# A fused attention and long-convolution kernel: sixteen transfers change from GpSimd's DMA queue to SyncE's

## The chip, the cores and the metric

The kernel runs on one core of a Trainium2 chip. The metric is the device time of one execution in microseconds. The engines are TensorE (PE; its weight loads are PEld), VectorE (DVE), ScalarE (ACT), GpSimd (POOL) and SyncE (SP). SP computes nothing here: it only waits and issues DMA transfers.

## The reference

Two independent blocks work on sequences of 2048 rows and 512 columns, and their results stand side by side in the output of 2048 x 1024.

```
A: qkv = x @ wqkv, 32 heads of 16
   a   = concat_heads(softmax(q k^T / 4) v) @ wo
B: k_shift = causal 4-tap filter of k, channel by channel
   kv  = k_shift * v
   y   = causal convolution of kv with ssm_k over all 2048 lags (by FFT in the reference) + kv * ssm_D
   b   = q * y
out = concat([a, b], axis=-1)
```

## The kernel before

The attention runs as a stream of chunks of two or three score blocks (128 keys by 512 queries). PE writes the scores (line 791), ACT takes the exponential of two or three blocks at once (line 798), and PE multiplies the result with v (line 866). Every second chunk or so one block's exponential is computed on DVE and POOL instead: DVE makes the integer part (line 817), POOL a linear term from it (line 290, into `EM` or `WKV`), and DVE three more passes (lines 826 and 827). Line 826 waits for POOL's result.

Between the chunks PE computes the long convolution as matmuls with Toeplitz tiles (line 998). Each of 512 channels has one tile `WR` of 128 x 2048, read from the scratch tensor `kz_scratch` (512 KB each). Fourteen tiles are held at a time. Four channels make one group ("quad"), 128 quads in all. When PE has finished quad n, SP may issue the four loads that overwrite its tiles, those of the channels 14 to 17 beyond the quad's first. So SP waits for PE once in four loads, and issues in the order of the program.

Each time 32 channels are done, PE turns the result and DVE multiplies it with q into `QN` (line 1038). `QN` holds one half of the channels: after eight turns it is stored (the first half of output B), and after that store has landed the second half of q is fetched into the same tile. The second half is stored near the end.

The attention's output projection (line 940) runs for each block of 512 queries once its heads are done. DVE copies each of its four 128 x 512 results to `OUTA` (line 952), a ring of three, and a DMA stores it (`op_out`). So a copy waits until the store three before it has landed. The last four results are stored otherwise (`op_out_end`), by SP and ACT, from `QT`. The weights of the projection are fetched into half of `WKV` at about 155 us (`load_wop`), once PE has done the last use of the weights that lay there.

All DMA transfers go through the helper `dma(eng, dsem, outp, inp, deps)`, whose first argument is the engine that waits for `deps` and issues; the profile gives each of them line 367. The order on every engine is fixed when the program is built. A planner with costs chooses the order of DVE's jobs; a store is appended to its issuing engine's list when the DVE job that makes its data is placed.

Of the kernel before, what the change touches and what calls it, by code (L numbers as in the profile page):

```python
# [13 lines left out]
D = 512  # L14
# [17 lines left out]
R_A = 3  # L32
# [139 lines left out]
def bass_concat_heads__mha_block__ssm_conv_h3__prompt_kernel(  # L172
# [12 lines left out]
    x2, q2, k2, v2, out2 = A_x[0], B_q[0], B_k[0], B_v[0], out[0]  # L185
# [8 lines left out]
    def sem(name):  # L194
        return enter(nc.semaphore(name))

    def sb(name, shape, dt=BF16):
        return enter(nc.sbuf_tensor(name, shape, dt))
# [10 lines left out]
    QN = sb("QN", [128, NB, 256])  # L209
# [7 lines left out]
    OUTA = sb("OUTA", [128, R_A, D])  # L217
# [10 lines left out]
    def xn(t):  # L228
# [5 lines left out]
    WOP = WKV[:, 0, :, :]  # L234
# [14 lines left out]
    pe, act, dve, pool, sp = [Eng(sem(n), *k) for n, k in (("s_pe", (170.0,)), ("s_act", (100.0,)), ("s_dve", (-10.0, -85.0)),  # L249
                                                           ("s_pool", ()), ("s_sp", ()))]  # L250
# [89 lines left out]
    def pe_op(fn, deps, mms):  # L340
        advance(pe.t)
        return pe.op(fn, [force(d) for d in deps], cost=Mm(*mms))

    def dve_op(fn, deps=(), cost=692.0):
        return dve.op(fn, [force(d) for d in deps], cost=cost)
# [3 lines left out]
    def dve_job(fn, deps, cost=692.0, slack=900.0, then=None, two=False):  # L349
        if dyn[0]:  # L350
            j = job(fn, deps, cost, pe.t + slack + cost, then)
            j.two = two
            return j
        h = dve_op(fn, deps, cost)
        if then:
            then(h)
        return h

    def full(n, k):
        return [("full", 0, n)] * k  # L360

    def dma(eng, dsem, outp, inp, deps=(), transpose=False):
        h = dsem.add()

        def fn(e):
            f = e.dma_start_transpose if transpose else e.dma_start
            f(outp, inp).then_inc(dsem.sem, 16)  # L367
        eng.op(fn, deps, inc=False)
        return h
# [5 lines left out]
    d_tap, d_kz, d_kzw, d_wo = [DmaSem(sem(n)) for n in ("d_tap", "d_kz", "d_kzw", "d_wo")]  # L375
    d_q = [DmaSem(sem(f"d_q{i}")) for i in range(2)]
    d_outB = [DmaSem(sem(f"d_outB{i}")) for i in range(2)]
    d_outE = DmaSem(sem("d_outE"))
    d_outA = [DmaSem(sem(f"d_outA{i}")) for i in range(R_A)]
# [212 lines left out]
    def kv_chunk(j):  # L592
        b = kvbuf[kv_buf[j]]
        st = {}

        def tap(m):
            in1 = TB[:, m:m + 1, :].broadcast_to([128, 2, D])
            st[m] = dve_job(lambda e: e.tensor_tensor(b[m], b[m], in1, ALU.mult),
                            [h_kv[(j, 0)], h_kv[(j, 1)], h_tb[m]], 750.0, 3000.0)

        def add(m):
            st["a"] = dve_job(lambda e: e.tensor_tensor(b[3], b[3], b[m], ALU.add), [st[m], st[3], st.get("a")], 750.0, 3500.0)

        def last():
            def then(h):
                h_kvfree[j] = h
                nxt = {4: 1, 3: None, 2: 0}.get(j, j - 3)
                if nxt is not None and nxt >= 0:
                    load_kv(nxt)
                for d in {6: (0, 1), 5: (2, 3), 4: (4, 11), 3: (8, 9, 12, 13), 1: (5, 6, 7)}.get(j, ()):  # L610
                    load_wr(d, [h])
                if j == 5:
                    load_qn(0, [h_kzt[0]], 4, NB)
                    line[0] += 5000.0
                elif j == 0:
                    start_conv(h)
            for i in range(2):
                dve_job(lambda e, i=i: e.tensor_tensor(KV[:, :, NB - 1 - 2 * j - i, :], quads(b[3][:, i, :]), quads(b[4][:, i, :]), ALU.mult),  # L618
                        [st["a"], h_xt[0]], 460.0, 4000.0 + i, then if i else None)
        return [lambda m=m: tap(m) for m in (3, 2)] + [lambda: add(2), lambda: tap(1), lambda: add(1),  # L620
                                                       lambda: tap(0), lambda: add(0), last]
# [60 lines left out]
    for c in range(4):  # L682
        h = turn_first([c], 2, h_xn[0])
        src = PS[:, first_bank[c], :].bitcast(BF16)[:, 0:512]
        if c == 1:
            hh = act.op(lambda e, c=c, src=src: e.activation(xT[:, c, 0:512], src, ACT.Copy), [h], cost=515.0)
        else:
            hh = dve_op(lambda e, c=c, src=src: e.tensor_copy(xT[:, c, 0:512], src), [h], 390.0)
# [237 lines left out]
    h_outa = {}  # L926
    op_count = [0]
    h_wop = [None]

    def load_wop(h_last):  # L930
        h_wop[0] = dma(pool, d_wo, WOP, A_wo.rearrange("(o p) f -> p o f", p=128), [h_last])

    def op_mm(qb, t, j0, j1, bank):
        dd = [bank_free[bank] if j0 == 0 else None, h_wop[0]]
# [10 lines left out]
    def op_out(qb, t, bank, h, slack):  # L945
        i = op_count[0]
        op_count[0] += 1
        r0 = qb * QB + t * 128

        def store(hh):  # L950
            h_outa[i] = dma(pool, d_outA[i % R_A], out2[r0:r0 + 128, 0:D], OUTA[:, i % R_A, :], [hh])
        bank_free[bank] = dve_job(lambda e: e.tensor_copy(OUTA[:, i % R_A, :], PS[:, bank, :]),  # L952
                                  [h, (lambda: h_outa.get(i - R_A, WAIT)) if i >= R_A else None], slack=slack, then=store)
        h_op[(qb, t)] = h
# [11 lines left out]
    h_wr, h_wrfree, h_qn = {}, {}, {}  # L966
# [11 lines left out]
        h_wr[d] = dma(sp, d_wr[r], WR[:, r, :], src, deps)  # L978

    def load_qn(i, deps, t0, t1):  # L980
        h_qn[i] = dma(pool, d_q[0], QN[:, t0:t1, :],
                      q2[128 * t0:128 * t1, 256 * i:256 * i + 256].rearrange("(t p) d -> p t d", p=128), deps)

    def conv_lags(qd, n0, n1):
# [34 lines left out]
    def conv_turn(b, bank, slack):  # L1019
        pbf = PS[:, bank, :].bitcast(BF16)  # L1020

        def fn(e):
            ins = None
            for k in range(4):
                ins = e.transpose(pbf[:, 128 * k:128 * k + 128], YB[:, b % 2, 128 * k:128 * k + 128], IDN[:, :])
            return ins
        h = pe_op(fn, [bank_free[bank], h_yb_in[b], h_idn], full(128, 4))
        h_yb[b] = h
        sl = b // 8
        yv = bass.AP(tensor=pbf.tensor, offset=pbf[:, NB - 1:NB].offset, ap=[pbf.ap[0], [-1, NB], [NB, CHB]])  # L1030
        qv = QN[:, :, CHB * (b % 8):CHB * (b % 8) + CHB]

        def store(hh):
            dst = out2[:, D + 256 * sl:D + 256 * (sl + 1)].rearrange("(t p) c -> p t c", p=128)
            ho = dma(pool, d_outB[0], dst, QN[:, :, :], [hh])
            if sl == 0:
                dve_later.append((len(chunks) + 14, lambda: load_qn(1, [ho], 0, NB)))
        bank_free[bank] = dve_job(lambda e: e.tensor_tensor(qv, yv, qv, ALU.mult), [h, lambda: h_qn.get(sl, WAIT)],
                                  slack=slack, then=store if b % 8 == 7 else None)
# [16 lines left out]
    def start_conv(h):  # L1056
        h_kvc[0] = h
        state["started"] = True
        load_wr(10, [h])
        load_qn(0, [h], 0, 4)  # L1060
        now = at_of(h)
        state["dma"] = max(line[0], now) + 5000.0
        state["wr"] += [now - 1000.0, max(line[0], now) + 2000.0, state["dma"] - 1400.0]
        state["dma"] -= 1400.0
# [16 lines left out]
    def run_unit(T, kind, u):  # L1081
        bank = 3 * (T % 2) + 2
        late = at_of(h_exp[T]) - pe.t - 800.0
        if kind == "u":
            state["u"] += 1
            evac_unit(u, bank, pe_unit(u, bank), slack=late - (Q_FIRST if u[0] == "q" else 0.0))
            if u[0] == "q":
                flow["half"] = max(flow["half"], T + Q_GAP)
            if u == ("k", 3, 3):
                load_wop(pe_last())  # L1090
        elif kind == "turn":
            state["turned"] += 1
            conv_turn(u, bank, late)
            if u == 7:
                state["dma"] += 8000.0
                state["wr"] = [t + 8000.0 if t > at_of(h_exp[T]) else t for t in state["wr"]]
        else:
            state["op"] += 1
            op_out(*u, bank, op_mm(*u, 0, 4, bank), slack=late)
# [303 lines left out]
```

## Time and profile before

| what | us |
|---|---|
| median of 3 runs | 847.1 |
| lowest and highest run | 843.85, 848.3 |
| time of the profiled execution | 848.2 |
| span of the profiled execution (first to last instruction) | 846.4 |
| ACT busy | 819.2 (97%) |
| DVE busy | 798.4 (94%) |
| PE busy | 719.9 (85%) |
| POOL busy | 290.6 (34%) |

In the profile, "idle before, releaser" names what ended an engine's idle time. A row of the waits reads: who waited, for whom, microseconds in total, times, longest. A row of the timeline reads: start, length, engine, line, operation, and in brackets the idle time ahead of it and what ended that. "SPq" is SP's list of instructions. "Landing" is the time from a DMA's issue to the last of its data.

### The profile page before, as it was taken

The page shows a single profiled execution, that of the slowest core. Times are in us where ns is not written, and L with a number is a line of the kernel's source. Part 1 is how long each engine was busy: PE and PEld are TensorE (multiplying, and loading weights), DVE is VectorE, ACT ScalarE, POOL GpSimd, SP SyncE. Part 2 cuts the span into 40 slices and gives each one's busy share as a digit, 9 for nine tenths or more (in the row PEclk, how much of TensorE's full clock was granted, in tenths as well). Part 3 has the DMA queues.
Part 4 walks back from the last instruction along what each step waited for, and adds up shares of the span by engine and source line. Part 5 has one row for each costly group of instructions (what it writes and reads, how often), then busy time and mean ns, then how long its engine had stood idle before and what let it go on. Part 6 is the DMA issues. An engine that isn't in the chain of part 4 may idle for free.

```text
span 846.4 us, 29917 instructions
## 1 busy us (share of the span) xinstructions
PE 719.9 (85%) x13144; PEld 310.1 (37%) x13144; DVE 798.4 (94%) x1346; ACT 819.2 (97%) x732; POOL 290.6 (34%) x323
## 2 busy tenths in 40 slices
PE   8999888888888888888888888888888988888897
PEld 3322333433343343333333333333333343333332
DVE  3998899999999999999999899999999999999996
ACT  6998999999999999999999899999999999999997
POOL 3232233334333333333333433333332334333431
PEclk9999999999999999999999999999999999999999
DMA  9878699999999999999998999999999999999810
GB/s 325 302 266 291 219 405 351 382 407 406 387 351 389 387 408 382 386 359 389 386 381 303 374 365 407 366 409 377 359 343 363 374 411 384 380 395 387 342 51 26
DMA packets 88867, 295.69 MB, mean 349 GB/s; under 512 B 11173, under 2 KB 19362, under 8 KB 88482
## 3 DMA queue, kind: packets, MB, share of 16 engines
q1 hardware_dynamic: 82818, 280.00, 87.5%
q0 software_dynamic: 3776, 12.58, 4.2%
q8 instruction: 105, 1.72, 0.8%
q10 hardware_dynamic: 2144, 1.18, 0.5%
q14 instruction: 24, 0.20, 0.1%
HBM read 287.31 MB, written 6.42 MB: 347 GB/s over the span
## 4 chain that ended last, share of the span: by engine, by line
ACT 71%; PE 13%; DVE 12%; issue 2%; DMA 1%; POOL 1%; ACTq 0%; DVEq 0%
ACT PT L798 71%; PE PS L791 5%; PE PS L866 2%; DVE PTD L827 2%; DVE EM L826 2%; DVE EI L817 2%; PE PS L521 2%; DVE WKV L826 2%; PE PS L998 1%; PE PS L940 1%; DMA WKV<-in_A_wqkv_dram 1%; DVE OUTA L952 1%; PE PS L507 1%; PE PS L514 1%; DMA QT<-in_B_k_dram 1%
## 5 line engine op out<-in xcount | busy, mean ns | idle before, releaser
L798 ACT ACTIVATE PT<-PS 128x1024 bf16<-128x1024 f32 (+1 forms) x726 | 815.6, 1328 | 16.4 <-PE PS L791 14.8
L791 PE MATMUL PS<-QT,KTo 32*128 32x512 bf16 x2048 | 287.4, 387 | 113.3 <-ACT PT L798 92.8
L998 PE MATMUL PS<-WR,KVP 128*30 128x128 bf16 (+15 forms) x8192 | 258.7, 222 | 4.7 <-issue 4.2
L998 PEld LDWEIGHTS PS<-WR,KVP 128*29 128x29 bf16 (+15 forms) x8192 | 178.2, 95 | 79.7 <-issue 40.4
L290 POOL TENSOR_SCALAR EM<-EI 128x512 f32<-128x512 uint16 x131 | 126.9, 969 | 224.3 <-DVE WKV L826 114.8
L290 POOL TENSOR_SCALAR WKV<-EI 128x512 f32<-128x512 uint16 x130 | 125.9, 969 | 208.8 <-DVE EM L826 100.3
L866 PE MATMUL PS<-PT,VAF 128*32 128x512 bf16 x1787 | 188.6, 394 | 1.8 <-issue 0.7
L817 DVE TENSOR_SCALAR EI<-PS 128x512 int32<-128x512 f32 x261 | 177.3, 679 | 7.0 <-PE PS L791 6.7
L826 DVE SCALAR_TENSOR_TENSOR EM<-EM 128x512 f32<-128x512 f32 x262 | 175.0, 683 | 2.3 <-POOL EM L290 2.0
L826 DVE SCALAR_TENSOR_TENSOR WKV<-WKV 128x512 f32<-128x512 f32 x260 | 173.1, 682 | 2.0 <-POOL WKV L290 1.8
L791 PEld LDWEIGHTS PS<-QT,KTo 32*128 32x128 bf16 x2048 | 71.8, 91 | 275.3 <-ACT PT L798 218.2
L827 DVE SCALAR_TENSOR_TENSOR PTD<-EI,EM 128x512 uint16<-128x512 int32 x131 | 89.1, 681 | 0.4
L827 DVE SCALAR_TENSOR_TENSOR PTD<-EI,WKV 128x512 uint16<-128x512 int32 x130 | 88.2, 679 | 0.3
L866 PEld LDWEIGHTS PS<-PT,VAF 128*32 128x32 bf16 x1787 | 47.4, 93 | 109.1 <-issue 99.0
L866 PE MATMUL PS<-PTD,VAF 128*32 128x512 bf16 x261 | 79.2, 394 | 0.3
L1120 PE MATMUL PS<-IDN,ZER 128*32 128x512 bf16 x396 | 44.1, 382 | 0.0
L892 DVE STREAM_TRANSPOSE DT<-PS 128x512 f32<-128x512 f32 x31 | 22.1, 712 | 8.4 <-PE PS L866 8.2
L866 PEld LDWEIGHTS PS<-PTD,VAF 128*32 128x32 bf16 x261 | 19.8, 95 | 19.6 <-issue 8.1
L542 DVE TENSOR_TENSOR QT<-PS,MSK 128x1024 bf16<-128x1024 f32 x15 | 18.3, 1222 | 4.0 <-PE PS L507 3.9
L521 PE MATMUL PS<-WKV,xT 128*128 128x512 bf16 x64 | 19.2, 384 | 0.1
L367 POOL DMA_DIRECT2D out_dram<-OUTA x12 | 7.1, 593 | 34.8 <-DVE OUTA L952 34.8
L367 POOL DMA_DIRECT2D WR<-in_B_k_dram x15 | 11.0, 737 | 22.8 <-DVE KVP L618 14.8
(80 smaller groups left out, 295.2 us busy)
## 6 DMA issues: line engine op xcount, KB each, us to landing
WR<-kz_scratch SPq DMA_DIRECT2D x512, 512.0 KB, 8.0
WR<-in_B_k_dram POOLq DMA_DIRECT2D x15, 256.0 KB, 7.4
kz_scratch<-WR SPq DMA_DIRECT2D x4, 544.0 KB, 6.6
out_dram<-QN POOLq DMA_DIRECT2D x2, 1024.0 KB, 7.9
QT<-in_B_k_dram POOLq DMA_DIRECT2D x7, 256.0 KB, 6.2
out_dram<-OUTA POOLq DMA_DIRECT2D x12, 128.0 KB, 5.7
WR<-in_B_v_dram SPq DMA_DIRECT2D x5, 256.0 KB, 8.5
WR<-in_B_k_dram SPq DMA_DIRECT2D x5, 256.0 KB, 10.4
```

Of the source, the lines that this page charges most:

```text
L290: q.h = pool.op(lambda e: e.tensor_scalar(UB[m % len(UB)], f, PA, PB, ALU.mult, ALU.add), [h, fx.h, free], cost=Beside((h[0], h[1] + 1)))
L521: return e.matmul(PS[:, bank, :], lhsT=xT[:, dc, kt * 128:(kt + 1) * 128], rhs=WV[:, dc, :], start=(dc == 0), stop=(dc == 3))
L542: hh = dve_job(lambda e: e.tensor_tensor(QT[:, qb % 2, 2 * o:2 * o + 2, :], src, MSK[:, :, 0:1].broadcast_to([128, 2, QB]), ALU.mult), [h, ...
L791: ins = e.matmul(PS[:, bank, :], lhsT=KTo[32 * s:32 * s + 32, g // 2, kt * 128:(kt + 1) * 128], rhs=QT[32 * s:32 * s + 32, qb % 2, g, :], ...
L798: h_exp[T] = act.op(lambda e: e.activation(PT[:, T % R_PT, 0:n * QB], PS[:, banks[0]:banks[0] + n, :].rearrange("p b f -> p (b f)"), ACT.E ...
L817: h_fix[i] = job(lambda e: e.tensor_scalar(ei, PS[:, bank, :], FIX_LO, FIX_ADD, ALU.max, ALU.add), [h, h_pair.get(i - 4)], 692.0, end)
L826: js.append(job(lambda e, c=c: e.scalar_tensor_tensor(u, u, c, u, ALU.add, ALU.mult), [js[-1]], 693.0, due + 700.0 * (len(js) - 3)))
L827: js.append(job(lambda e: e.scalar_tensor_tensor(PTD[:, i % 4, :].bitcast(UINT16), ei, 2.0 ** -9, u, ALU.mult, ALU.add), [js[2], (lambda: ...
L866: ins = e.matmul(PS[32 * s:32 * s + 32, pvb(qb * NG + g), :], lhsT=VAF[:, kt, h * VW:h * VW + 32], rhs=rhs, start=first[b], stop=last[b], ...
L892: h_t = dve_job(lambda e: e.transpose(out=dt, in_=PS[:, pvb(n), :]), [h, h_mult.get(n - 2 if n == 2 else n - 1) if n != 1 else None], 717. ...
L998: ins = e.matmul(PS[32 * c:32 * c + m * NB - n, BGB, 128 * kk:128 * kk + 128], lhsT=KVP[:, o:o + 4 * (m * NB - n) - 3:4], rhs=WR[:, d % R_ ...
L1120: ins = e.matmul(PS[32 * s:32 * s + 32, pvb(n), :], lhsT=ZER[:, 0:32], rhs=IDN[:, :].rearrange("p (a f) -> p a f", a=1).broadcast_to([128, ...
```

## The change

Fourteen stores (twelve of `OUTA`, two of `QN`), the fetch of the second half of q and the fetch of the projection's weights are issued by SP instead of POOL. The first half of q stays with POOL. The second fetch gets a semaphore of its own. Both halves of `QN` are still stored on the same semaphore.

```diff
     def load_wop(h_last):
-        h_wop[0] = dma(pool, d_wo, WOP, A_wo.rearrange("(o p) f -> p o f", p=128), [h_last])
+        h_wop[0] = dma(sp, d_wo, WOP, A_wo.rearrange("(o p) f -> p o f", p=128), [h_last])
...
         def store(hh):
-            h_outa[i] = dma(pool, d_outA[i % R_A], out2[r0:r0 + 128, 0:D], OUTA[:, i % R_A, :], [hh])
+            h_outa[i] = dma(sp, d_outA[i % R_A], out2[r0:r0 + 128, 0:D], OUTA[:, i % R_A, :], [hh])
...
     def load_qn(i, deps, t0, t1):
-        h_qn[i] = dma(pool, d_q[0], QN[:, t0:t1, :],
+        h_qn[i] = dma(sp if i else pool, d_q[i], QN[:, t0:t1, :],
                       q2[128 * t0:128 * t1, 256 * i:256 * i + 256].rearrange("(t p) d -> p t d", p=128), deps)
...
             dst = out2[:, D + 256 * sl:D + 256 * (sl + 1)].rearrange("(t p) c -> p t c", p=128)
-            ho = dma(pool, d_outB[0], dst, QN[:, :, :], [hh])
+            ho = dma(sp, d_outB[0], dst, QN[:, :, :], [hh])
```

The instructions of PE, ACT and DVE keep their order; POOL's and SP's change. On POOL, at about 250 us, where the first four results of the projection are stored (`out_dram<-OUTA`), among the linear terms (`EM<-EI`, `WKV<-EI`):

```order
-L290 TENSOR_SCALAR WKV<-EI 128x512
-L367 DMA out_dram<-OUTA 128x512
-L290 TENSOR_SCALAR WKV<-EI 128x512
-L290 TENSOR_SCALAR EM<-EI 128x512
-L367 DMA out_dram<-OUTA 128x512
-L290 TENSOR_SCALAR EM<-EI 128x512
-L367 DMA out_dram<-OUTA 128x512
-L290 TENSOR_SCALAR WKV<-EI 128x512
-L367 DMA out_dram<-OUTA 128x512
-L290 TENSOR_SCALAR WKV<-EI 128x512
+L290 TENSOR_SCALAR WKV<-EI 128x512 x2
+L290 TENSOR_SCALAR EM<-EI 128x512 x2
```

The four stores are gone from between the linear terms, which now stand directly behind each other.

On SP, in the stretch from the quad that is computed at about 440 us (the loads `WR<-kz_scratch` run through it) to 470 us, with the first half's store of output B (`out_dram<-QN`), the second block's four stores and the second fetch of q (`QN<-in_B_q_dram`), in the changed kernel:

```order
+L367 DMA WR<-kz_scratch 128x2048 x132
+L367 DMA out_dram<-QN 128x16x256
+L367 DMA out_dram<-OUTA 128x512 x2
+L367 DMA WR<-kz_scratch 128x2048 x4
+L367 DMA out_dram<-OUTA 128x512
+L367 DMA QN<-in_B_q_dram 128x16x256
+L367 DMA WR<-kz_scratch 128x2048 x4
+L367 DMA out_dram<-OUTA 128x512
+L367 DMA WR<-kz_scratch 128x2048 x136
```

Where there was one unbroken row of loads, the stores and the fetch now stand between quads of loads. SP must have seen each one's wait end before it comes to the next four loads.

## The prediction

> **What bounds the kernel now.** I read the page's busy shares first, then its chain of waits and ACT's own group, and then the waits.
>
> ```profile
> span 846.4 us, 29917 instructions
> PE 719.9 (85%) x13144; PEld 310.1 (37%) x13144; DVE 798.4 (94%) x1346; ACT 819.2 (97%) x732; POOL 290.6 (34%) x323
> ACT 71%; PE 13%; DVE 12%; issue 2%; DMA 1%; POOL 1%; ACTq 0%; DVEq 0%
> L798 ACT ACTIVATE PT<-PS 128x1024 bf16<-128x1024 f32 (+1 forms) x726 | 815.6, 1328 | 16.4 <-PE PS L791 14.8
> ```
>
> ACT's exponentials set the time. ACT was idle for only 16.4 us ahead of its 726 exponentials, nearly all of it behind PE's scores. So nothing gets more than 2% faster without a shorter exponential, and whatever delays PE by more than its small lead over ACT makes the kernel slower. POOL has room, but DVE, at 94%, waits for POOL's linear terms. The DMA transfers matter in two ways: POOL spends time issuing them, and the convolution's tiles (`WR`) must land before PE comes to them.
>
> **What POOL gives up.** Each group's median issue on POOL, and the same kind of store as SP already issues it at the end:
>
> ```profile
> L367 POOL DMA_DIRECT2D out_dram<-OUTA x12: 588/588/608, 251.1 to 674.4; - x12
> L367 POOL DMA_DIRECT2D out_dram<-QN x2: 1219/1225/1231, 447.1 to 816.6; - x2
> L367 SPq DMA_DIRECT2D out_dram<-QT x2: 338/338/338, 843.0 to 843.6; - x2
> ```
>
> POOL loses 12 x 0.59 + 2 x 1.23 = 9.5 us of issuing, and about 2 us more for the two fetches. That alone is worth nothing, as POOL is idle two thirds of the time. What counts is that the linear term behind a store in POOL's list must wait until the store's data are there. At the first store this reads so (DVE, then POOL, then DVE again):
>
> ```profile
> 250.16 0.69 DVE L952 CAST OUTA<-PS 128x512 bf16<-128x512 f32 x1
> 251.15 0.61 POOL L367 DMA_DIRECT2D out_dram<-OUTA  x1 [3.54 <-DVE OUTA L952]
> 251.83 0.70 POOL L290 TENSOR_SCALAR WKV<-EI 128x512 f32<-128x512 uint16 x1
> 252.56 0.69 DVE L826 SCALAR_TENSOR_TENSOR WKV<-WKV 128x512 f32<-128x512 f32 x1 [0.51 <-POOL WKV L290]
> ```
>
> POOL sat idle for 3.54 us ahead of the store, and the linear term came 0.08 us behind its end. DVE then lost 0.51 us on it. Without the store the term may start in that idle time, and the 0.51 us go. The same shape stands behind five stores: the whole of DVE's waits for POOL from 90 to 830 us is
>
> ```profile
> DVE WKV L826 <- POOL WKV L290: 1.8, 4, 0.5
> DVE EM L826 <- POOL EM L290: 1.3, 2, 0.7
> 464.11 0.69 DVE L826 SCALAR_TENSOR_TENSOR EM<-EM 128x512 f32<-128x512 f32 x1 [0.51 <-POOL EM L290]
> ```
>
> The four on `WKV` all follow a store (at 252.56, 266.80, 661.43 and 675.68 us), and so does the one at 464.11; the other, 0.7 us, stands at the start of the DVE blocks, far from any store. So 1.8 + 0.51 = 2.3 us of DVE's idle time go. DVE is not the engine that bounds the time, so I look at what ACT lost within 4 us behind such a wait:
>
> ```profile
> 256.23 1.45 ACT L798 ACTIVATE PT<-PS 128x1536 bf16<-128x1536 f32 x1 [0.17 <-PE PS L791]
> 466.73 1.02 ACT L798 ACTIVATE PT<-PS 128x1024 bf16<-128x1024 f32 x1 [0.46 <-PE PS L791]
> 665.11 1.45 ACT L798 ACTIVATE PT<-PS 128x1536 bf16<-128x1536 f32 x1 [0.20 <-PE PS L791]
> ```
>
> That is 0.17 + 0.46 + 0.20 = 0.8 us. The bounds are 0, if these came from PE's own order, and 2.3 us, if every moment of DVE counted. I take 0.8, since ACT is where the time is made.
>
> **What SP takes on.** SP issues in order, so a store that waits for DVE holds up the loads behind it. Whether that costs anything depends on which ends later: the store's data, or the PE quad for which the loads wait anyway. SP's waits, then its next load behind the first, fourth and fifth `OUTA` store and the first `QN` store, with POOL's rows of these stores (POOL started 0.3 us after the data were there):
>
> ```profile
> SPq L367 <- PE PS L998: 311.7, 86, 13.1
> 250.88 0.32 SPq L367 DMA_DIRECT2D WR<-kz_scratch  x1
> 265.50 0.59 POOL L367 DMA_DIRECT2D out_dram<-OUTA  x1 [4.10 <-DVE OUTA L952]
> 269.07 0.32 SPq L367 DMA_DIRECT2D WR<-kz_scratch  x1
> 447.13 1.22 POOL L367 DMA_DIRECT2D out_dram<-QN  x1 [2.82 <-DVE QN L1038]
> 453.55 0.60 POOL L367 DMA_DIRECT2D out_dram<-OUTA  x1 [3.24 <-DVE OUTA L952]
> 444.58 15.48 SPq L367 DMA_DIRECT2D WR<-kz_scratch  x5
> ```
>
> The last row holds the load at 444.58 and the four that start at 458.2: SP waited 13.1 us for PE there, the longest of its waits, and the `QN` store at 447 and the two `OUTA` stores fall inside it. At 265.50 there are 3.6 us to spare. The tightest is the first: the copy ended at 250.16 + 0.69 = 250.85, 0.03 us ahead of the load. There the load moves back by one issue, 0.34 us. I went through all sixteen in this way, the fetch of the weights too (POOL at 154.66, SP's next load at 155.97), and no other data came later than the wait that is there now. So SP is not held up by them while the timing stays as it is, and a load that comes 0.34 us late is covered by the lead of the loads over PE. The nearest rows for that lead, at the two places with another transfer:
>
> ```profile
> WR<-kz_scratch SPq DMA_DIRECT2D x1, 512.0 KB, 10.3
> 167.44 0.23 PE L998 MATMUL PS<-WR,KVP 128*32 128x128 bf16 x3
> WR<-kz_scratch SPq DMA_DIRECT2D x1, 512.0 KB, 10.1
> 478.71 0.31 PE L998 MATMUL PS<-WR,KVP 128*32 128x128 bf16 x1
> ```
>
> The first pair is the load issued at 156.34 behind the fetch of the weights: it landed at 166.6 and was used at 167.44, 0.8 us later. The second is the load issued at 465.15 behind the second fetch of q: it landed at 475.25, used at 478.71, a lead of 3.5 us. In both cases the other transfer's bytes were already moving in the same microseconds (it took 9.3 and 10.4 us to land, below), so putting them ahead of the loads in one queue adds no bytes to what must move before the loads have landed. I cost this at nothing; without that cover it is rival two.
>
> ```profile
> WR<-kz_scratch SPq DMA_DIRECT2D x512, 512.0 KB, 8.0
> out_dram<-OUTA POOLq DMA_DIRECT2D x12, 128.0 KB, 5.7
> WKV<-in_A_wo_dram POOLq DMA_DIRECT2D x1, 512.0 KB, 9.3
> QN<-in_B_q_dram POOLq DMA_DIRECT2D x1, 1024.0 KB, 10.4
> DMA to landing us min/median/max: 2.9/8.0/14.1
> ```
>
> Last, a copy to `OUTA` waits for the store three before it. From POOL these land in 5.7 us, the loads of SP's queue (last row) in 8.0, at worst 14.1. The fourth copy of a block begins some 13 us behind the end of the first (the fourth copy ends at 265.2, the first at 250.85, less 0.7 for the copy itself), so even 13 us would do: nothing lost.
>
> The sum: 848.2 us of the profiled execution, less 0.8, is 847.4. That execution lies 1.1 us above the median of the runs; against the median of 847.1 it is 846.3.
>
> The Trainium skill, on the page "DMA: Bandwidth & Descriptors", section "Issuing engines are not separate DMA queues", says that all issuers feed the same 16 DMA engines and that choosing another one only saves issue time on a sequencer. By it alone the sum would be the 847.1 of before; the trace shows the wait behind the store besides, which the rule does not speak of.
>
> **Rival one: more of ACT's idle time goes.** Near the three groups of stores (250 to 275, 445 to 482 and 658 to 680 us) ACT waited, in this order,
>
> ```profile
> ACT PT L798 <- PE PS L791: 0.6, 2, 0.4
> ACT PT L798 <- PE PS L791: 3.1, 5, 1.8
> ACT PT L798 <- PE PS L791: 0.4, 2, 0.2
> 474.77 0.22 PE L998 MATMUL PS<-WR,KVP 128*8 128x128 bf16 x1 [2.27 <-issue]
> 475.00:480.00 5.00, 5.00 (x86) 2.08 (x86) 3.00 (x6) 4.04 (x4) 1.20 (x2) 0.66 1.03 415
> ```
>
> If the second fetch of q on a queue of its own is what held PE for 2.27 us at 472.5 (a stall behind which the granted clock was 0.66 in the next 5 us), all 4.1 us go: 843.0, just within half a per cent, and faster by more only if a little else goes too. Against it: a stall of the same kind ("issue") of 1.7 us stands at 612 us, with no transfer of POOL's near.
>
> **Rival two: the loads queue behind the fetch of q, slower.** The second fetch is 1 MB. Alone in its queue it shares the DMA engines with the loads; in SP's queue the loads issued at 464.8 and after wait for all of it. If the loads then need the fetch's whole 10.4 us on top of their own 10.1, the load issued at 465.15 lands at 485.65, 6.9 us after PE wants it at 478.71. PE and then ACT stand still for that time, and PE restarts at a lower clock as behind the stall above. At 475.25 + 3.5 us it begins to cost; in full it gives 847.1 + 6.9 = 854.0. For it: the DMA engines are full there (share 1.03 in the row above), so nothing can be caught up quickly. Against: those 10.4 us were spent beside the loads, not alone, so the true addition is smaller, down to nothing. The Trainium skill, same page, section "Queues, rings and completion order", states that each DMA engine takes turns packet by packet between the queues that have work. By that rule the fetch loses its turns, and the loads behind it lose theirs until it is through; the trace agrees so far as POOL's stores land in 5.7 us against 8.0 for SP's loads. No run here shows such a fetch in SP's queue.
>
> **How the numbers follow.** About half a per cent, 4.2 us, is what a measurement of this kernel can tell from no change (three runs lie 4.5 us apart). The first case gets 0.60; its own range, 843 to 850, is the gain of 0 to 2.3 us with the spread of the runs. Rival one gets 0.12, as the stall at 472 may be of PE's own making; I put all of it on "faster", with what little else it needs. Rival two gets 0.28: SP's list is the one that feeds the convolution, its queue is full, and the lead is only 3.5 us. The range from 843.0 to 853.5 holds the first case, half of rival one and nearly all of rival two.
>
> **What would show it.** Right: DVE's waits for POOL behind stores are gone; SP's loads behind stores start within 0.4 us of PE's release; ACT's idle time ahead of line 798 is about 15.6 us. Rival one: no stall of PE near 472 us and ACT's idle time near 12 us. Rival two: PE's line 998 late at about 478 us for DMA, with idle time on ACT just behind it. The prediction is wrong if SP waits for DVE for more than 2 us ahead of any load, or if a store in SP's list takes several microseconds to issue.

## The result and the profile after

The changed kernel takes 841.89 us (median of 20 runs, 838.2 to 862.48) against 846.53 us for the kernel before (20 runs, 842.5 to 865.08). The ratio is 0.9952, with a 95% interval from 0.9935 to 0.997: faster by 0.3 to 0.65%, and 1.1 us below the lower end of the range that was given. The longest run of each (862.48 and 865.08 us) fell into a slower state; such runs are left out of every ratio and of all that is worked out from the clock below. The profiled execution took 842.7 us.

The page of the changed kernel: span, busy shares, chain of waits, and ACT's exponentials with their idle time.

```profile
span 840.8 us, 29871 instructions
PE 710.1 (84%) x13098; PEld 310.1 (37%) x13144; DVE 797.5 (95%) x1346; ACT 818.2 (97%) x732; POOL 283.7 (34%) x307
ACT 72%; DVE 14%; PE 9%; issue 2%; DMA 1%; POOL 1%; ACTq 0%; DVEq 0%
L798 ACT ACTIVATE PT<-PS 128x1024 bf16<-128x1024 f32 (+1 forms) x726 | 814.6, 1338 | 11.1 <-PE PS L791 9.5
```

ACT's exponentials take as long as before (814.6 us against 815.6); its idle time ahead of them fell from 16.4 to 11.1 us, and the span by 5.6 us. So most of the time came from ACT's waits for PE. These are one trace of each kernel; in a second trace of each (h4 and h8 below) the idle time was 13.8 and 9.3 us. (46 matmuls of 13144 are missing from the changed kernel's trace, so PE's smaller busy time says nothing.)

DVE's waits for POOL from 90 to 830 us in the changed kernel, all that is left of them:

```profile
DVE EM L826 <- POOL EM L290: 1.5, 2, 0.7
```

These two stand at 94.8 and 828.3 us, where no store is near. Both were there before; the second then stood at 833.9 us, outside the stretch.

The timeline at the first store, POOL's row, then DVE's, then SP's:

```profile
250.05 1.00 POOL L290 TENSOR_SCALAR WKV<-EI 128x512 f32<-128x512 uint16 x1 [2.00 <-DVE WKV L826]
250.60 0.69 DVE L952 CAST OUTA<-PS 128x512 bf16<-128x512 f32 x1
251.80 1.28 DVE L826 SCALAR_TENSOR_TENSOR WKV<-WKV 128x512 f32<-128x512 f32 x2
251.31 0.34 SPq L367 DMA_DIRECT2D out_dram<-OUTA  x1
251.70 1.45 SPq L367 DMA_DIRECT2D WR<-kz_scratch  x3
```

The linear term now starts 0.55 us before the copy to `OUTA`, where it came 1.7 us after its start, and DVE's line 826 runs twice without a gap. SP's store begins as soon as its data are there and the loads follow 0.05 us behind it. All five waits behind stores are gone.

The second place is the second fetch of q. SP's timeline there in the changed kernel:

```profile
461.06 0.56 SPq L367 DMA_DIRECT2D QN<-in_B_q_dram  x1
463.04 4.76 SPq L367 DMA_DIRECT2D WR<-kz_scratch  x4
```

The same loads in the kernel before (the fourth stands in its next row):

```profile
464.79 1.27 SPq L367 DMA_DIRECT2D WR<-kz_scratch  x3
```

And PE behind its stall in the changed kernel:

```profile
471.99 0.22 PE L998 MATMUL PS<-WR,KVP 128*8 128x128 bf16 x1 [1.23 <-issue]
```

The fetch itself is issued in 0.56 us, but the first load behind it took SP 3.3 us (four loads from 463.04 to 467.80, where three took 1.27 us before). From the changed kernel's DMA view, with the median time from issue to landing at the end of each row:

```profile
QN<-in_B_q_dram SPq DMA_DIRECT2D x1, 1024.0 KB, 8.2
out_dram<-OUTA SPq DMA_DIRECT2D x12, 128.0 KB, 6.4
```

The fetch landed in 8.2 us where it took 10.4 on POOL's queue. PE's stall at that place is 1.23 us instead of 2.27. ACT's waits for PE at the three groups of stores were 0.6, 3.1 and 0.4 us before; in the changed kernel the profile shows none at the first and the third, and at the second

```profile
ACT PT L798 <- PE PS L791: 1.4, 3, 0.7
```

That is 4.1 - 1.4 = 2.7 us less of ACT's waits at the places that the change touches, about half of what ACT's idle time lost between these two traces.

**The granted clock.** Each run comes with the clock that TensorE was granted. Over 280 runs of the kernels shown here (112 of them of the kernel before, run beside the experiments), a line through each kernel's runs with one common slope gives 0.68 us of time (standard error 0.02) for each microsecond of clock lost, lost clock being (1 - clock) x time. The traces show where it is lost: in windows of 3.4 us at half clock, at times two or more in a row. So a window (1.7 us lost) costs some 1.15 us, an estimate from that slope. Put at full clock, the kernel before takes 841.5 us and the changed one 838.8: a difference of 2.75 us, plus or minus 0.57 (95%, as all such figures here). The other 1.7 us of the mean difference are lost clock (0.68 x 2.5 us): 7.3 us a run before, 4.8 after, about 4.3 windows and 2.8. That part is the less certain one: with the standard errors of the table the 2.5 us are known to about 1.9. The table uses the same line for every timed kernel; the middle column is the work's own time, the last the clock. It compares each kernel with all 112 runs of the kernel before. These came in four groups, one beside each set of experiments, and the groups differ by up to 0.9 us at full clock (841.0 to 841.9). Against the group beside it, the rows move by some 0.3 us or less, but for two: h5 gains only 1.0 +- 0.9 and h6 loses 0.6 +- 0.9. The difference between these two stays 1.5 +- 1.0 us.

| kernel | ratio (95% interval) | at full clock, against before, us | clock lost, us a run (std. error) |
|---|---|---|---|
| before | 1 | 0 | 7.3 (0.3) |
| the change | 0.9952 (0.9935 to 0.997) | -2.75 +- 0.57 | 4.8 (0.9) |
| e1: OUTA stores alone | 0.9975 (0.9954 to 0.9996) | -1.79 +- 0.68 | 6.2 (0.9) |
| e2: QN stores and fetch of q alone | 0.9966 (0.9942 to 0.9991) | -1.54 +- 0.68 | 5.6 (1.0) |
| e3: fetch of the weights alone | 0.9991 (0.9968 to 1.0013) | -0.07 +- 0.68 | 6.7 (0.7) |
| e4: all on POOL, stores one place later | 0.9994 (0.9965 to 1.0024) | -1.93 +- 0.68 | 8.6 (1.5) |
| g1: the change, fetch of q earlier | 0.9954 (0.993 to 0.9977) | -2.41 +- 0.70 | 3.7 (1.0) |
| g2: before, without the fetch of q | 0.9996 (0.9971 to 1.0022) | -0.17 +- 0.68 | 8.0 (0.8) |
| g3: fetch of q alone | 1.0002 (0.9974 to 1.003) | -1.56 +- 0.68 | 8.9 (1.0) |
| g4: QN and fetches on SP, OUTA as e4 | 0.9927 (0.9898 to 0.9955) | -3.55 +- 0.79 | 3.6 (0.7) |
| h1: g4, at most five loads under way | 0.9917 (0.989 to 0.9944) | -3.50 +- 0.71 | 2.3 (0.5) |
| h2: before, at most five loads under way | 0.9986 (0.9961 to 1.0011) | -0.74 +- 0.68 | 6.5 (0.6) |
| h3: before, three loads held 1.6 us | 1.0013 (0.9988 to 1.0038) | +0.62 +- 0.68 | 6.7 (0.5) |
| h5: before, loads held 3.6 us | 0.9985 (0.9956 to 1.0014) | -1.54 +- 0.74 | 5.2 (1.0) |
| h6: fetch of q on SP, behind the loads | 0.9996 (0.9972 to 1.002) | 0.00 +- 0.74 | 5.7 (1.0) |

### The profile page after: what moved, and what is told of

The parts are those of the page before. It is cut to its first block, busy times and chain, and to the rows that moved or that the text cites. A ratio compares the mean times of both kernels' runs of the same rounds, so it can differ in the third digit from the quotient of the medians.

```text
span 840.8 us, 29871 instructions
## 1 busy us (share of the span) xinstructions
PE 710.1 (84%) x13098; PEld 310.1 (37%) x13144; DVE 797.5 (95%) x1346; ACT 818.2 (97%) x732; POOL 283.7 (34%) x307
## 3 DMA queue, kind: packets, MB, share of 16 engines
q10 hardware_dynamic: 2144, 1.18, 0.5%
## 4 chain that ended last, share of the span: by engine, by line
ACT 72%; DVE 14%; PE 9%; issue 2%; DMA 1%; POOL 1%; ACTq 0%; DVEq 0%
ACT PT L798 72%; PE PS L791 3%; DVE EI L817 3%; DVE PTD L827 2%; DVE EM L826 2%; PE PS L866 2%; DVE WKV L826 2%; PE PS L521 1%; DMA WKV<-in_A_wqkv_dram 1%; PE PS L998 1%; DVE DT L892 1%; PE PS L507 1%; PE PS L514 1%; PE PS L940 1%; DMA QT<-in_B_k_dram 0%
## 5 line engine op out<-in xcount | busy, mean ns | idle before, releaser
L798 ACT ACTIVATE PT<-PS 128x1024 bf16<-128x1024 f32 (+1 forms) x726 | 814.6, 1338 | 11.1 <-PE PS L791 9.5
L290 POOL TENSOR_SCALAR EM<-EI 128x512 f32<-128x512 uint16 x131 | 129.2, 986 | 243.8 <-DVE WKV L826 122.4
L290 POOL TENSOR_SCALAR WKV<-EI 128x512 f32<-128x512 uint16 x130 | 128.2, 986 | 235.0 <-DVE EM L826 106.9
L998 PEld LDWEIGHTS PS<-WR,KVP 128*30 128x30 bf16 (+15 forms) x8192 | 177.9, 95 | 77.5 <-issue 37.7
L558 DVE CAST VAF<-PS 128x512 bf16<-128x512 f32 x16 | 11.0, 689 | 7.1 <-PE PS L521 7.1
```

What stands on the lines that cost most here:

```text
L290: q.h = pool.op(lambda e: e.tensor_scalar(UB[m % len(UB)], f, PA, PB, ALU.mult, ALU.add), [h, fx.h, free], cost=Beside((h[0], h[1] + 1)))
L798: h_exp[T] = act.op(lambda e: e.activation(PT[:, T % R_PT, 0:n * QB], PS[:, banks[0]:banks[0] + n, :].rearrange("p b f -> p (b f)"), ACT.E ...
L998: ins = e.matmul(PS[32 * c:32 * c + m * NB - n, BGB, 128 * kk:128 * kk + 128], lhsT=KVP[:, o:o + 4 * (m * NB - n) - 3:4], rhs=WR[:, d % R_ ...
```

## The experiments: which part brings it

Theory one was that POOL's linear terms no longer stand behind a store that waits for its data. Theory two was that fewer stalls and half-clock windows of PE come with the transfers' leaving POOL's queue. All kernels keep the order of PE's, ACT's and DVE's instructions.

**e1**, **e2** and **e3** each move one part.

```diff
 e1:  h_outa[i] = dma(sp, d_outA[i % R_A], ...)       # was pool
 e2:  ho = dma(sp, d_outB[0], dst, QN[:, :, :], [hh])  # was pool
      h_qn[i] = dma(sp if i else pool, d_q[i], ...)    # was pool, d_q[0]
 e3:  h_wop[0] = dma(sp, d_wo, WOP, ...)               # was pool
```

> Only the twelve stores of OUTA go to SP; the stores of QN, the second fetch of q and that of the weights stay with POOL. Theory one (POOL's linear terms no longer wait behind a store for its data): nearly the whole gain, a ratio to the kernel before of 0.995 to 0.997, four of the five waits of DVE for POOL behind stores gone and ACT's idle time ahead of line 798 down by 1 to 3 us. Theory two (fewer stalls and half-clock windows of PE once the large transfers around QN leave POOL's queue): a ratio of 0.998 to 1.000.

> Only the two stores of QN and the second fetch of q go to SP. Theory one: a ratio of 0.999 to 1.001, and DVE's waits for POOL behind OUTA stores stay, 1.8 us on WKV. Theory two: 0.995 to 0.997, and PE's stall at 472 us gone or shorter than 1.3 us.

> Only the fetch of the projection's weights goes to SP. Theory one and theory two alike: a ratio of 0.999 to 1.001, ACT's idle time unchanged up to 250 us. If the time moves by more than 0.2%, neither theory is enough, and the time hangs on something that any change of the transfers' timing moves.

Medians were 844.17, 843.67 and 845.53 us against 846.31. So neither theory alone: the OUTA stores and the QN part each give about half (1.8 and 1.5 us at full clock), and the fetch of the weights nothing that can be told from zero. In e1's trace all five of DVE's waits behind stores are gone. In e2's they stayed, as theory one says, and yet e2 gained.

**e4** asks whether the gain of the stores needs another queue. The store stays with POOL, but behind the linear term that stood after it.

```diff
-            h_outa[i] = dma(pool, d_outA[i % R_A], ..., [hh])
+            h_outa[i] = d_outA[i % R_A].add(); held.append((the same store, [hh]))
...  # emit_linear, behind the linear term; the QN stores in the same way
+        [pool.op(f, d, inc=False) for f, d in held]; held.clear()
```

> All transfers stay with POOL, but each store of OUTA and QN is put behind the linear term that stood after it. Theory one: as the whole change, a ratio of 0.995 to 0.997, DVE's waits for POOL behind stores gone. Theory two: 0.999 to 1.001, since the queue of every transfer is that of before.

The median was 844.38 us. The ratio, 0.9994, cannot be told from 1 and by itself would speak for theory two, but these runs lost more clock than any but g3's. At full clock the gain is 1.93 us, that of e1. The trace shows why. From 90 to 830 us DVE's waits for POOL are the same two as in the changed kernel, and POOL's timeline has the linear term ahead of the first store:

```profile
250.73 1.00 POOL L290 TENSOR_SCALAR WKV<-EI 128x512 f32<-128x512 uint16 x1 [2.00 <-DVE WKV L826]
252.27 0.61 POOL L951 DMA_DIRECT2D out_dram<-OUTA  x1 [0.54 <-DVE OUTA L952]
```

**g4** puts both together: QN and both fetches on SP as in the change, OUTA stores on POOL as in e4.

> The stores of QN and both fetches go to SP as in the change, but the OUTA stores stay with POOL, each behind the linear term that stood after it. If the gain of the OUTA part is that the linear terms are released, whatever queue the store takes: ratio 0.994 to 0.997, as the whole change. If it is SP's queue that matters for these stores: 0.996 to 0.998, as with the QN part alone.

The median was 840.52 us, ratio 0.9927, and 3.55 us at full clock. So the OUTA part needs the order on POOL, not the other queue. The mixed kernel is at least as fast as the change; the intervals of the two ratios overlap.

## The experiments: what the fetch of q does

The QN part had no price in the prediction but a loss, so the next kernels take it apart. **g1** issues the fetch six chunks earlier, **g2** leaves it out of the kernel before, **g3** moves it alone.

```diff
 g1 (on the change):  dve_later.append((len(chunks) + 8, lambda: load_qn(1, [ho], 0, NB)))   # was 14
 g2 (on before):      h_qn[1] = ho                                                           # no fetch
 g3 (on before):      h_qn[i] = dma(sp if i else pool, d_q[i], ...)
```

> The whole change, with the second fetch of q six chunks earlier, so that SP issues it at about 456 us, ahead of the four loads of 457 us, where the DMA engines have nothing to do. If PE's stall at 472 us (its instructions arrive late while the DMA engines are full) comes from the fetch's bytes beside the loads: the stall and ACT's idle 0.7 us there gone, ratio to the kernel before 0.993 to 0.995, a little faster than the whole change. If the stall is PE's own: ratio 0.995 to 0.996, stall as in the changed kernel (1.2 us).

> The kernel before, without the second fetch of q (left out: the second half of B is multiplied with what the first left in the tile). If the fetch's bytes delay PE's instructions: no stall of PE at 472 us, ratio 0.996 to 0.998, as much as moving the QN transfers to SP gave. If they do not: the stall stays at 1.5 to 2.3 us and the ratio is 0.999 to 1.001.

> Only the second fetch of q goes to SP; the stores of QN and all else stay with POOL. If it is the fetch that matters in the QN part: ratio 0.996 to 0.998 and a shorter stall at 472 us. If it is the QN stores, or the wait behind them on POOL: 0.999 to 1.001.

Medians were 841.46, 846.72 and 846.55 us (before: 846.92). The fetch's bytes are not it: without the fetch PE still stalled for 1.98 us there and nothing was gained. Issued earlier, ahead of another four loads, the fetch helped no more than at its place: PE stalled for 1.24 us. g3 was unclear by its time, since its runs lost 8.9 us of clock; at full clock it gained 1.56 us, all that e2 did, and its trace has no stall of over 0.6 us there.

What differs is SP's next load. In g3 the first load behind the fetch took SP 3.9 us to issue, and the other three came after it (fetch, then three of the loads):

```profile
460.80 0.49 SPq L367 DMA_DIRECT2D QN<-in_B_q_dram  x1
465.48 4.88 SPq L367 DMA_DIRECT2D WR<-kz_scratch  x3
```

So the next loads were issued about 3 to 4 us later than before. PE's stall ends behind a fetch of instructions, taken to be PE's own and seen in the DMA view of 472 to 473.4 us of the kernel before, 16 KB, and at 474.77 us PE went on:

```profile
q1 hardware_dynamic: 88, 0.30, 55.0%
q0 software_dynamic: 75, 0.23, 42.4%
q8 instruction: 1, 0.02, 4.4%
```

In every trace each stall of PE of over 1 us without a releaser ("issue") ended 1.2 to 1.6 us after the end of such a fetch. From this came a third theory: the hold on the loads, not the fetch's queue, spares PE the stall, because its instructions then do not wait behind as many loads.

**h1** and **h2** limit the loads under way to five, in the mixed kernel and in the kernel before. **h3** holds three loads until an earlier one has landed. **h4** is the kernel before, for a second trace.

```diff
 h1, h2:  h_wr[d] = dma(sp, d_wr[r], WR[:, r, :], src, deps + ([h_wr[d - 5]] if d >= 20 else []))
 h3:      h_wr[d] = dma(sp, d_wr[r], WR[:, r, :], src, deps + ([h_wr[272]] if d == 275 else []))
```

> The mixed kernel (QN and both fetches on SP, OUTA stores on POOL behind the linear terms), and each load of a convolution tile also waits until the load five before it has landed, so that at most five are under way. If PE's stalls without a releaser and its half-clock windows come from its instructions waiting behind a deep backlog of loads: fewer of them, ratio 0.988 to 0.992. If not, or if the lead of the loads is used up: 0.993 or more, with idle time of PE on line 998.

> The kernel before with the same limit of five loads under way, nothing moved. If the backlog of loads is behind the stalls: no stall of PE at 472 and 605 to 614 us, ratio 0.993 to 0.997. If not: 0.999 or more.

> The kernel before with one wait more: the load that SP issues at 465.1 us waits until the one issued at 459.1 has landed, some 4 us later, as it was held back behind the second fetch of q where that was in SP's queue. If this hold is what spared PE the stall at 472 us: the stall gone, time at full clock 1 to 2 us less, ratio 0.996 to 0.999. If it was something else in the fetch's move: the stall stays, ratio 0.999 to 1.001.

> The kernel before once more, for a second trace: the five waits of DVE for POOL behind stores come back to within 0.1 us each, while the half-clock windows of PE stand elsewhere, if their place is a matter of chance.

Medians were 839.06, 845.79 and 846.67 us (before: 846.92), the second trace's time 846.08. The limit of five did little for the kernel before, and the stall stayed at 2.0 us; on the mixed kernel it gave the lowest time of all, 0.9917, though no more at full clock than g4, and its trace has a stall of 1.24 us where g4's has none. h3 failed: it held the loads for only 1.6 us of the 4 that were meant, and the stall stayed at 2.0 us. In h4 the five waits came back to within 0.1 us, and a stall of 2.00 us stood at 473.79; its half-clock windows stood at 475 and 611 us, the latter of twice the length, those of the first trace at 356, 476, 605, 616 and 793.

So two kernels more: **h5** holds all loads from that place on for as long as the fetch did, without the fetch's move, and **h6** moves the fetch but behind those loads.

```diff
 h5 (on before):  h_wr[d] = dma(sp, d_wr[r], WR[:, r, :], src, deps + ([h_wr[273]] if d == 274 else []))
 h6 (on g3):      dve_later.append((len(chunks) + 20, lambda: load_qn(1, [ho], 0, NB)))       # was 14
```

> The kernel before, where all loads from the one of 464.8 us on wait until the load of 459.5 has landed, about 3.2 us: the hold that SP's list had behind the second fetch of q, without that fetch's move. If the hold spares PE the stall: no stall near 472 us, or one under 1.3 us, and ACT's idle time there down from 1.5 to under 0.8 us. If not: a stall of 2 us, as in the two traces of the kernel before.

> Only the second fetch of q on SP, but six chunks later, behind the four loads of 465 us, so that these are not held. If the hold spares PE the stall: the stall of 2 us is back near 472 us. If it is enough that the fetch is off POOL: no stall, as with the fetch at its place in SP's list.

> The kernel with only the second fetch of q on SP once more, for a second trace. If the missing stall at 472 us belongs to the kernel: missing again. If it is chance: 1 to 2 us of stall.

> The changed kernel once more, for a second trace. The stall at 472 us again 1.2 us and ACT's idle time there 0.7 us, if they belong to the kernel; the half-clock windows elsewhere than before, two to four of them.

Medians were 842.86 and 845.3 us (before: 845.52), the single runs of h7 and h8 took 842.04 and 840.24. The timeline of h4 where PE goes on behind its stall:

```profile
473.79 0.22 PE L998 MATMUL PS<-WR,KVP 128*8 128x128 bf16 x1 [2.00 <-issue]
```

Of h5, SP's held loads, then the same place on PE:

```profile
467.68 1.52 SPq L367 DMA_DIRECT2D WR<-kz_scratch  x3
472.96 0.22 PE L998 MATMUL PS<-WR,KVP 128*8 128x128 bf16 x1 [1.18 <-issue]
```

Of h6:

```profile
473.19 0.27 PE L998 MATMUL PS<-WR,KVP 128*8 128x128 bf16 x1 [1.98 <-issue]
```

Of h7, the second trace of g3:

```profile
473.21 0.22 PE L998 MATMUL PS<-WR,KVP 128*8 128x128 bf16 x1 [0.61 <-issue]
```

And of h8, the second trace of the changed kernel:

```profile
473.02 0.22 PE L998 MATMUL PS<-WR,KVP 128*8 128x128 bf16 x1 [1.23 <-issue]
```

The hold alone (3.6 us in its trace) shortens the stall to 1.18 us and gains 1.54 us at full clock, as much as the fetch's move (1.0 +- 0.9 against the runs beside it). The fetch on SP without the hold leaves 1.98 us and gains nothing. The ratios of both (0.9985 and 0.9996) cannot be told from 1, so this rests on the stalls, one trace each, and on the times at full clock. ACT's waits at the three groups of stores say the same, in h5:

```profile
ACT PT L798 <- PE PS L791: 0.6, 2, 0.4
ACT PT L798 <- PE PS L791: 1.4, 3, 0.7
ACT PT L798 <- PE PS L791: 0.4, 2, 0.2
```

and in h6:

```profile
ACT PT L798 <- PE PS L791: 0.6, 2, 0.4
ACT PT L798 <- PE PS L791: 2.5, 3, 1.7
ACT PT L798 <- PE PS L791: 0.4, 2, 0.2
```

In both the first and the third group are those of before, as no OUTA store was moved. The middle one fell from 3.1 to 1.4, the value of the changed kernel, where the loads were held, and only to 2.5 where they were not; in the other traces without that hold and with the stores on POOL it lies between 1.9 and 3.1. The second traces repeat: g3's stall is short again (0.61 us, where the first had none of over 0.6 us), and the changed kernel's is 1.23 us in both.

The hold is enough to shorten the stall, but it is not the only way. In g1 the four loads of this place were not held, and yet:

```profile
462.01 1.83 SPq L367 DMA_DIRECT2D WR<-kz_scratch  x4
470.96 0.22 PE L998 MATMUL PS<-WR,KVP 128*8 128x128 bf16 x1 [1.24 <-issue]
```

e1, with the fetch still on POOL, has 1.51 us. Nor does the backlog explain it: when the instruction fetch came, 7, 6 and 5 loads were under way in the traces of before, g2 and h2, with stalls of 2.0 to 2.3 us, and 7, 6 and 5 in those of the change, h5 and h1, with 1.2. What goes with the stall in all eighteen traces is when the instruction fetch starts, counted from PE's first weight load of the convolution in the last batch ahead of the stall (471.75 us in the kernel before). It starts 0.2 to 0.6 us behind it in the eight traces that stall for 1.7 to 2.3 us, 0.15 to 0.4 us ahead of it in the six that stall for 1.2 to 1.5 us, and 1.3 to 2 us ahead of it in the four with at most 0.6 us. Why the hold makes the fetch come earlier is open.

What stays open as well is the clock. The kernels with the least clock lost are those with both parts in them (the change, g1, g4, h1: 2.3 to 4.8 us a run); with one part it is 5.2 to 8.9. Many windows stand at places that no edit touches (356 and 793 us), and between the single parts the differences are mostly within two standard errors. At the one place that the experiments do touch, stall and window go together: each of the seven traces that stall for 1.98 us or more has a half-clock window that begins within 1.6 us of the stall's end, and none of the eleven with a shorter stall has one there. That would be one window, some 1.15 us, of what the clock gave. No experiment changed the clock alone, so how much of the 1.7 us comes from it was not shown.

## Why the prediction was wrong

**POOL gives up the stores: mechanism right, size too small.** The wait behind the store was read rightly, and all five waits of DVE are gone. The step that failed is the term of 0.8 us: it counted only what ACT lost within 4 us behind such a wait. e1 and e4 gave 1.8 and 1.9 us at full clock (each +- 0.7). In the first and third group all of ACT's waits went, 1.0 us where 0.37 had been counted; the 0.46 us at 466.73 that had been counted as well stayed (0.46 us in h8's trace at the same place). The likely reason is that a late DVE is late for every later bank that it frees, not only for the next; no run shows this by itself, and the traces do not say where the rest of the 1.8 us stood. The measured gain lies inside the bounds of 0 to 2.3 us that were given for this term.

**SP takes on the stores: right.** SP's waits in the changed kernel:

```profile
SPq L367 <- PE PS L998: 279.4, 85, 7.1
SPq L367 <- DVE OUTA L952: 21.4, 10, 5.5
```

SP does wait for DVE, for up to 5.5 us, but in time in which it waited for PE before (311.7 us in all), and no wait of a store for its data held the loads up beyond that: at the first store, the tightest, the next load came 0.05 us behind the store's issue. The projection's stores land in 6.4 us instead of 5.7, and no copy waited for one. So the other queue made little difference to them; the 5.7 us against 8.0 of the prediction compared stores of 128 KB with loads of 512 KB.

**The fetch of q costs nothing: wrong in sign.** Rival two's mechanism did take place: the loads were held behind the fetch, by 3.3 us. Its price failed. It put the fetch's 10.4 us on top of the load's own 10.1. Measured from the fetch's issue to the landing of the second load behind it, this took 11.8 us (461.06 to 472.9) where it had taken 11.1 side by side (464.14 to 475.25), and PE used that load at 474.6, 1.7 us after it had landed. The sum itself counted the place at nothing. What it left out is that PE's stall there could shrink: it went from 2.27 to 1.23 us, and in e2, g3 and g4, with the fetch but not the `OUTA` stores on SP, to 0.6 us or less. The fetch alone gave some 1.5 us at full clock (g3), and the hold alone as much (h5).

**Rival one** came nearest, at 843.0: 2.7 of its 4.1 us of waits went, the stall among them in part, and ACT's idle time of 11.1 us is near the 12 that it named, not the 15.6 of the forecast. Its reason, the fetch on a queue of its own holding PE, was wrong: without the fetch PE stalled as long (g2).

**No term for the clock.** The forecast took the run's clock as given. The change lost 2.5 us less of it a run, worth 1.7 us. With the 2.75 us at full clock that makes 4.45 us, where 0.8 had been forecast. Why less clock was lost stays open.

## What to carry to other kernels

A transfer that waits for its data in a busy engine's list holds up what stands behind it in that list, and the engine that waits for that; either move the transfer or put it one place later, which cost nothing here and gave the same. Where the time of a kernel varies from run to run with the granted clock, compare kernels at equal clock as well: of thirteen parts and variants here, three that gained 1.5 to 1.9 us of work could not be told from no change by their times alone. And a load that is issued earlier is not always better: here loads held for 3 to 4 us still landed in time, and PE, which had stalled behind a fetch of instructions, stalled less.

## What the runs showed of the hardware

SP issues a load in 0.43 us in the median, but the load behind the 1 MB fetch of 2048 pieces of 512 bytes took 3.3 us in the changed kernel (the maximum in the second row below; the first is the kernel before), 3.7 in e2 and 3.9 in g3. In h6 it took 2.8 us and in g1, with the fetch earlier, 1.4. The `OUTA` store behind the first `QN` store took 1.5 us (the maximum in the third row). The fetch itself was issued in 0.4 to 0.65 us. So it is the next transfer in SP's list that pays.

```profile
L367 SPq DMA_DIRECT2D WR<-kz_scratch x512: 319/433/2032, 43.5 to 797.5; - x171
L367 SPq DMA_DIRECT2D WR<-kz_scratch x512: 319/433/3332, 44.3 to 792.1; - x171
L367 SPq DMA_DIRECT2D out_dram<-OUTA x12: 332/338/1496, 251.3 to 668.2; - x12
```

A half-clock window of 3.4 us cost some 1.15 us of this kernel's time, and by their clocks (0.982 to 1.0) the runs of the changed kernel lost the worth of 0 to 9 of them; both are estimates.
